# Six first products of batch 1 turned by DMA instead of computed transposed, row loads held by small copies, order refitted

## The chip, the cores and the metric

The kernel runs on one core of one Trainium2 chip. The metric is the device time of one execution in microseconds (us), median of several runs. The core has five engines that run at the same time, each with its own in-order instruction stream: TensorE (PE, matrix products, with its weight loads listed as PEld), VectorE (DVE), ScalarE (ACT), GpSimd (POOL) and SyncE (SP). POOL and SP mainly start DMA transfers here. Engines wait for each other and for transfers through semaphores. An engine that waits keeps everything behind it in its own stream waiting too.

## The reference

Two stages. First a sliding-window attention with sink keys: q, k and v are 4 batches x 8 heads x 768 positions x 64, every query sees the last 128 keys and the first 4 keys.

```python
scores = scale * np.matmul(q, k.transpose(0, 1, 3, 2))
keep = (pos[None, :] < 4) | ((rel >= 0) & (rel < 128))
a = softmax(np.where(keep, scores, -1e9))
x = np.matmul(a, v)            # then heads side by side: x is 3072 x 512
```

Then a dense mixture of four experts, all of them applied to all 3072 tokens:

```python
p = domain_probs / (domain_probs.sum(-1, keepdims=True) + 1e-9)
for e in range(4):
    h = np.maximum(x @ w1[e], 0.0)          # 512 -> 1024
    out += p[:, e:e + 1] * (h @ w2[e])      # 1024 -> 512
```

## The kernel before

**Units.** Everything on PE is in bf16. The tokens of a batch (768) are three pairs of 128-token blocks, so there are 12 pairs (b, g) with b = 0..3 and g = 0..2. One expert on one pair is a unit, written (b, g, e); there are 48. Nearly all units do their matrix products in a seven-product (Strassen-Winograd) form: in place of eight block products there are seven, in the order P1 P5 P6 P2 P7 P3 P4, over sums of blocks of weights and of tokens that DVE, POOL and ACT form beforehand. A unit has two matrix products, the first (x @ w1, with relu) and the second (@ w2).

**The first product, two ways.** Its result H must lie with the hidden index on the partitions, as the second product contracts over it.
- The plain way, `emit_fast` (products at L1208): weights are the stationary operand (128x128), tokens the moving one, so H comes out as it is needed. One of the seven products is 8 matmuls of 128 columns. Gating (relu and the factor p) is done on DVE at L1241, with a row of p copied to all partitions: a "gate tile" that SP loads (`load_gate`, L478) for each such unit.
- The turned way, `emit_turning` (products at L1320): tokens are stationary, weights move, and one product is 2 matmuls of 512 columns. H comes out with tokens on the partitions. There the factor p is one number per partition (`own_gates`, loaded and normalised once by `own_load` and `own_made`), so that gating is either relu and scale on ACT (L1338, L1341) or one step on DVE (L1345). The gated values go into two half buffers, X[0] and X[1], and when the four writes of a unit are done two DMA transposes issued by SP (L1301) turn X[0] and X[1] into H.

**The half buffers of a turned unit.** X[1] serves twice. Its memory first holds the intermediate c5, which is copied out of the accumulator after P5 (ACT, L1373, called "keep" below). DVE adds c5 and the running sum into the accumulator V (L1367, "both"), which frees the accumulator that P7 writes to. DVE then adds P7's result to c5 (L1382). At the end X[1] takes the gated results of P7 and of P4, and only after P4 can X[1] be turned. The next unit that is given this buffer may write its c5 into it only when that transposition has read it.

```python
c5 = X[1].rearrange("p f t n -> p (f t n)").bitcast(FP32).rearrange("p (f n) -> p f n", f=QF)
at["P7"] = at["P3"] = dve(n)                          # "both": P7 may go behind it
return sum(x[0] <= t["pe"] + REST for x in self.resting)   # halves(): which buffers count as free
```

**The planner.** The order of all instructions is written by a planner in the kernel itself, before anything runs: it keeps a clock per engine (`pe`, `act`, `dve`, `pool`, `sp`, `lands`), with fitted costs, and at each step emits what its clocks and due times favour. `later` and `flush` do the same for the steps of DVE and ACT. The real engines then follow the order written, and wait where the plan was too early. A turned unit is opened only when `halves()` finds two buffers whose planned transposition ends no later than `REST` behind PE's planned time. `LANDS` is added to that planned end. The planner gives "keep" no due time after that transposition: the semaphore alone holds it on the chip.

**Who is turned.** `OWN` = 2 says that turned units begin with batch 2; `TURNED_UNITS` = (4, 0) leaves out the first four units of batches 2 and 3: 20 units are turned. Their half buffers are lent from attention tiles that have come to rest (qkn after the last turn of batch 3, then onat and aT) and, after the last plain unit, from the gate tiles (`rest_gates`). Four gate tiles serve the 20 plain units that gate by row.

**Rows of q, k and v.** For each batch six blocks of q and k rows (`load_nat`, L251) and of v rows (`load_v`, L318) are loaded by POOL, 128 KB a transfer. SP then turns q and k by DMA (`turn_nat`, L263) ahead of the scores (L689 onwards). Attention outputs are turned by the same kind of transposition (`turn`, L791). For batches 2 and 3 a GpSimd copy of a freshly turned tile into the two-column tile `held` (L1703), once for each batch, keeps POOL from issuing the first row loads before the last turn of the batch before.

Of the kernel before, what the change touches and what calls it, by code (L numbers as in the profile page):

```python
# [16 lines left out]
def kernel(  # L17
# [12 lines left out]
    nc = tc.nc  # L30
# [23 lines left out]
    GROUPS = [  # L54
        [(0, 0, 2), (1, 1, 1)],
        [(1, 2, 1), (2, 2, 2), (3, 3, 1)],
        [(3, 4, 1), (4, 4, 2), (5, 5, 1)],
    ]

    NGATE = 4  # L60
    TURN_ABOUT = 1
    OWN = 2
    TURNED_UNITS = (4, 0)
    EXPERTS = {(1, 0): (0, 2, 1, 3), (1, 1): (3, 2, 1, 0), (1, 2): (3, 2, 1, 0), (2, 2): (2, 0, 3, 1), (3, 1): (3, 2, 1, 0)}
    FIRST = 1
    START = {0: (1, 0), 1: (0, 2), 2: (0, 0), 3: (1, 0)}
    MIX = 6
    SHARE_OF = (1.01, 0.92, 0.96)
    LEAD = (1.01, 0.99)
    DUE = 1.9  # L70
    LOW_PRODUCT = 2.9
    LOW_SECOND = 2.7
    HIGH_PRODUCT = 1.9
    EARLY = -0.01
    MASK = 5000
    GATE = 800
    GATE0 = 300
    FORM = 6000
    TOKEN = 3000
    MARGIN = 500  # L80
    HOLD = 0
    FULL = 7
    STEP0 = 0.03
    READY = 40
    REST = 3000
    LANDS = 0
    SCALED = 300
    SHARED = 2
    MARGIN1, MARGIN2 = 4000, 14000
    OWNED_READ = 152  # L90
    WIDE = 2
    OPEN = 2.5
    SOON = 34000
    NEARLY = 2
# [5 lines left out]
    ONE = 2  # L100
    HOLDS = 2
    MORE = 2
    BOTH = 1
    PAIR = 0
    OVER = 4
    ALONE = 2.0
    BEHIND = 1500
    CHORES = 3
    BIASED = 1
# [19 lines left out]
    def act(cols, *deps):  # L129
        at = max([t["act"], *deps])  # L130
        t["act"] = at + max(196, 68 + cols / 1.23)
        return at + max(350, 205 + cols / 1.2)

    def dve(cols, *deps, rate=0.96, fixed=157):
        at = max([t["dve"], *deps])
        t["dve"] = at + fixed - 85 + cols / rate
        return at + fixed + 35 + cols / rate

# [60 lines left out]

    landed = {}  # L200
    ROW = {64: 12.8, 128: 22.6, 256: 41.7, 512: 79.8, 1024: 156.2}

    def lands(key, rows, cols, *deps):
        issued = pool(0, *deps, fixed=880)
        at = max(t["sw"], issued + 1500)
        t["sw"] = at + rows * ROW[cols] / 16
        landed[key] = t["sw"] + 900
        moved.append([key, at, t["sw"], ROW[cols]])

# [249 lines left out]

    gate_sb = {}  # L460
    gate_tiles = [consts.tile([P, 2, 2, P], FP32, name=f"gates{i}") for i in range(NGATE // 2)]

# [8 lines left out]
    def load_gate(pair, e):  # L471

        i = len(gate_sb) % NGATE
        x = gate_tiles[i // 2][:, i % 2]
        if FIRST <= len(gate_sb) < NGATE:
            nc.vector.memset(x[0:1, 0, 0:1], 0.0)
            dve(1, fixed=150)
        nc.sync.dma_start(  # L478
            out=x.rearrange("p t n -> p (t n)"), in_=gate_rows[pair, e].rearrange("t n -> (t n)").partition_broadcast(P),
        )  # L480
        gate_sb[pair, e] = x
        sp(takes=300)

# [26 lines left out]
    for tb in (2, 3):  # L510
# [18 lines left out]
    LOW = 32768.0  # L529
    low = [lent[:, 5 * P:8 * P], lent[:, 8 * P:12 * P]]  # L530
    nc.vector.tensor_scalar(
        out=low[0].rearrange("p (n q) -> p n q", n=3)[:, 0::2], in0=two, scalar1=LOW, scalar2=-LOW, op0=ALU.mult, op1=ALU.add,
    )
    nc.vector.tensor_scalar(out=low[0][:, P:2 * P], in0=own, scalar1=-LOW, scalar2=None, op0=ALU.mult)
    nc.vector.memset(low[0][0:NSINK, 0:2 * P], 0.0)
    nc.vector.reduce_sum(
        out=sel2, in_=ident.rearrange("p (n c) -> p n c", c=32)[:, :, 0:2 * NSINK].rearrange("p n (a j) -> p n a j", a=2), axis=AX.X,
    )
    x = low[1].rearrange("p (n c q) -> p n c q", n=2, c=2)
    nc.scalar.activation(out=x[:, :, 0], in_=two, func=AF.Copy, scale=-LOW)  # L540
    nc.scalar.activation(out=x[:, :, 1], in_=two, func=AF.Copy, scale=LOW, bias=-LOW)
    mask0 = consts.tile([P, 3 * P], BF16, name="mask0")
    mask1 = consts.tile([P, 4 * P], BF16, name="mask1")
    made = []

    def make_mask(i):
        def run(engine):
            x = (mask0, mask1)[i]
            if i:
                nc.scalar.activation(out=x, in_=low[i], func=AF.Copy, scale=1 / LOW, bias=1.0)  # L550
                act(4 * P)
            else:
                nc.vector.tensor_scalar(out=x, in0=low[i], scalar1=1 / LOW, scalar2=1.0, op0=ALU.mult, op1=ALU.add)
                dve(3 * P)
            made.append(i)
        later(("dve", "act")[i], (24000.0, 11700.0)[i], 8000, run)
# [132 lines left out]
    def scores(b, hp, g, more=False):  # L689
# [10 lines left out]
        if biased:  # L700
            for ph in range(2):
                nc.tensor.matmul(sps[ph][:, 0:w], lhsT=ident, rhs=low[min(g, 1)], start=True, stop=False, skip_group_check=True)
            pe(2 * w, ready, n=2)
# [18 lines left out]
        if b == 0:  # L722
            part = join(2, masked)
        else:
            def mask_both(at):
                def run(engine):
                    nc.vector.tensor_mul(a, a, m[:, None, :].to_broadcast([P, 2, w]))  # L727
                    masked(dve(2 * w, rate=1.92))
                later("dve", at, MASK, run)
            part = join(2, mask_both)  # L730
        for ph in range(2):
            def run(engine, ph=ph):
# [8 lines left out]
                def mask_one(engine):  # L741
                    nc.vector.tensor_mul(a[:, ph], a[:, ph], m)
                    part(dve(w, rate=1.92))
# [216 lines left out]
    class Mixture:  # L960


        def __init__(self):
# [13 lines left out]
            mine = [u for u in self.order if u[0] >= OWN]  # L977
            self.turning = set(mine[TURNED_UNITS[0]:len(mine) - TURNED_UNITS[1]])
            self.gated = [u for u in self.order if u not in self.turning]
            self.G, self.resting = {}, []  # L980
            self.T, self.T_at, self.fast, self.finished = {}, {}, {}, set()
# [43 lines left out]
        def opened(self, b, g, e):  # L1025
# [11 lines left out]
            def complete(at):  # L1037
                self.H_at[b, g, e] = at
                self.finished.add((b, g, e))
                if (b, g) >= PAIRS[0]:  # L1040
                    self.waiting.append((b, g, e))
                    load_gates()
                    if not TURNED_UNITS[1] and self.gated[-1] == (b, g, e):
                        self.rest_gates()
# [39 lines left out]
        def emit_first(self, what, ready):  # L1084
# [56 lines left out]
            def run(engine):  # L1141
# [5 lines left out]
                part(at)  # L1147
            later("dve", end, GATE0, run)

# [32 lines left out]
        def emit_fast(self, u, m, ready):  # L1182
# [40 lines left out]
            def gated(dst, src, half_, ready, slack, slot=None, then=None):  # L1223
# [16 lines left out]
                def run(engine):  # L1240
# [5 lines left out]
                    if then:  # L1246
                        then(at)
                later("dve", ready, slack, run)

# [35 lines left out]
        def emit_turning(self, u, m, ready):  # L1285
# [47 lines left out]
            def gated(k, s, src, ready, slack, slot=None, then=None):  # L1333
                gate = own_gates[:, 2 * ((b - OWN) * NG + g) + s, e:e + 1]

                def run(engine):
                    if engine == "act":
                        nc.scalar.activation(out=src, in_=src, func=AF.Relu)  # L1338

                        def scaled(engine):  # L1340
                            nc.scalar.mul(X[k][:, :, s], src, gate)  # L1341
                            done(act(n))
                        later("act", act(n), SCALED, scaled)
                        return
                    nc.vector.tensor_scalar(out=X[k][:, :, s], in0=src, scalar1=0.0, scalar2=gate, op0=ALU.max, op1=ALU.mult)  # L1345
                    done(dve(n, fixed=OWNED_READ))

                def done(at):
                    if slot is not None:
                        take(slot, at)  # L1350
# [40 lines left out]
        def chore(self):  # L1391
# [40 lines left out]
            def form(engine):  # L1432
                x = steps.pop(0)
                x[0](*x[1:])
                at = dve(QF * P, self.stored[-1] if (b, g) == PAIRS[0] else 0.0, rate=1.92)
                if steps:
                    go(form, self.until(b, g, e, "P6 P7".split()[len(steps) == 2]))
# [128 lines left out]
        def emit_second(self):  # L1566
# [20 lines left out]
            def run(engine):  # L1587
                if e == 0:
                    nc.vector.tensor_scalar(out=dst, in0=op, scalar1=sc, scalar2=None, op0=ALU.mult)
                else:  # L1590
                    nc.vector.scalar_tensor_tensor(
                        out=dst, in0=op, scalar=sc, in1=dst, op0=ALU.mult, op1=ALU.add,
                    )
                acc_free[bank] = at = dve(Dout, fixed=218)
                if e == E - 1:
                    r = (2 * g + s) * P
                    nc.sync.dma_start(out=out[r:r + P, :], in_=dst)
                    self.stored.append(sp(at))
            later("dve", end, 400, run)
            self.since = 0  # L1600
# [36 lines left out]
    work = [sum(NFB * NDB * G * (1 if (b, g) < START[e] else 7 / 8) + NFB * NDB * G * (1 if (b, g) < PAIRS[0] else 7 / 8) for g in range(NG) for e in range(E)) for b in range(B)]  # L1637
    ahead, upto, loaded, wide, rowed = 0, 0.0, 0, 0, 0
    asked = []
# [22 lines left out]
    while mix.more() or att.more():  # L1662
# [28 lines left out]
        if x and t["pool"] < now + 1500 and free_ring(x):  # L1691
            loads.remove(x)
            x[0](*x[1:])
        if turns and (ahead < 2 or not mix.second) and landed.get(("qk", *turns[0]), 1e12) < now and (turns[0][0] <= ahead or turns[0][0] == ahead + 1 and not att.todo):
# [7 lines left out]
            if 0 < b < B - 1 and x[1] == NQB - 1:  # L1702
                nc.gpsimd.tensor_copy(out=held, in_=qkT[b][:, 1, NHP - 1, S - 2:S])  # L1703
                pool(2, turned_at[x])
                nat_loads(b + 1, range(NQB))
                turns += [(b + 1, tb) for tb in range(NQB)]
        flush(now)
        mix.tokens()
# [3 lines left out]
        if ahead + 1 < B and not att.more() and (ahead == 0 or (ahead + 1, 0) in turned_at) and (ahead == 0 or mix.done >= sum(work[:ahead]) * LEAD[ahead - 1]):  # L1712
            ahead += 1
            if ahead == 1:
                own_load()
            elif ahead == 2:
                own_made()
            att = Attention(ahead)
# [79 lines left out]
```

## Time and profile before

| | |
|---|---|
| time, median of 3 runs | 354.05 us (353.97 to 354.15) |
| span of the profiled execution | 351.9 us |
| time outside the span (354.05 less 351.9) | 2.15 us |
| PE busy | 346.2 us, 98% of the span |
| DVE, ACT, POOL busy | 282.8, 208.3, 71.6 us |
| granted TensorE clock | 1.000 |
| matmuls | 3721 |

The profiled execution has no device time of its own beside its span; the span plus 2.15 us is the median by construction, and sums of durations from the profile are set against that. A line of a group reads: line, engine, operation, output and input tiles, shapes, count, then total busy time in us, mean time of one in ns, idle time ahead of the group with what ended it. A PE line's duration of a matmul includes its passage through the array; matmuls that follow each other overlap, so the cost of one is the distance between starts. A line with "SPq" is the issue of a transfer and not its duration.

### The profile page before, as it was taken

The page shows a single profiled execution, that of the slowest core. Times are in us where ns is not written, and L with a number is a line of the kernel's source. Part 1 is how long each engine was busy: PE and PEld are TensorE (multiplying, and loading weights), DVE is VectorE, ACT ScalarE, POOL GpSimd, SP SyncE. Part 2 cuts the span into 40 slices and gives each one's busy share as a digit, 9 for nine tenths or more (in the row PEclk, how much of TensorE's full clock was granted, in tenths as well). Part 3 has the DMA queues.
Part 4 walks back from the last instruction along what each step waited for, and adds up shares of the span by engine and source line. Part 5 has one row for each costly group of instructions (what it writes and reads, how often), then busy time and mean ns, then how long its engine had stood idle before and what let it go on. Part 6 is the DMA issues. An engine that isn't in the chain of part 4 may idle for free.

```text
span 351.9 us, 9351 instructions
## 1 busy us (share of the span) xinstructions
PE 346.2 (98%) x3721; PEld 266.0 (76%) x3721; DVE 282.8 (80%) x672; ACT 208.3 (59%) x476; POOL 71.6 (20%) x89
## 2 busy tenths in 40 slices
PE   8999999999999999999999999999999999999996
PEld 3685769656789998998999886755856676666685
DVE  5886999878999999799898999578768586675740
ACT  6863624447874443647453539689589767666611
POOL 8946114330546206100152000000000000000000
PEclk9999999999999999999999999999999999999999
DMA  9999999999999999920999602545437733545441
GB/s 178 178 188 195 223 214 181 179 160 174 162 147 165 121 145 122 132 64 9 109 173 159 113 32 62 120 101 120 80 91 174 127 89 93 120 120 115 67 120 61
DMA packets 161032, 45.61 MB, mean 130 GB/s; under 512 B 144740, under 2 KB 156996, under 8 KB 160988
## 3 DMA queue, kind: packets, MB, share of 16 engines
q0 software_dynamic: 79104, 17.31, 56.4%
q1 hardware_dynamic: 80828, 27.18, 40.1%
q8 instruction: 29, 0.48, 0.5%
q10 hardware_dynamic: 1056, 0.52, 0.5%
q14 instruction: 15, 0.12, 0.1%
HBM read 38.39 MB, written 6.34 MB: 127 GB/s over the span
## 4 chain that ended last, share of the span: by engine, by line
PE 75%; DMA 19%; POOL 5%; issue 1%; ACT 0%; POOLq 0%; SPq 0%
PE acc L1493 35%; PE cps L1320 17%; PE cps L1208 15%; DMA w<-in_moe_w_dram 12%; DMA qkn<-in_k_dram 4%; DMA qkT<-qkn 3%; PE sps L708 3%; PE od L774 2%; POOL qkn L251 2%; POOL w L331 1%; POOL vx L318 1%; PE hps L1118 1%; PE od L767 1%; POOL w L341 0%; PE acc L1579 0%
## 5 line engine op out<-in xcount | busy, mean ns | idle before, releaser
L1493 PEld LDWEIGHTS <-H 128*128 128x128 bf16 x708 | 66.5, 98 | 17.9 <-issue 1.1
L1493 PE MATMUL acc<-w,H 128*128 128x256 bf16 x420 | 56.9, 273 | 0.0
L733 ACT ACTIVATE aT<-sps 128x512 bf16<-128x512 f32 (+1 forms) x96 | 47.2, 579 | 16.3 <-PE sps L708 16.2
L1208 PEld LDWEIGHTS <-w 128*128 128x128 bf16 x640 | 39.1, 98 | 1.2 <-issue 0.5
L1493 PEld LDWEIGHTS <-S 128*128 128x128 bf16 x320 | 30.3, 98 | 9.5 <-issue 0.8
L1241 DVE SCALAR_TENSOR_TENSOR H<-cps,gates 128x512 bf16<-128x512 f32 x54 | 36.6, 683 | 0.0
L1338 ACT ACTIVATE cps<-cps 128x512 f32<-128x512 f32 x44 | 25.5, 585 | 17.5 <-PE cps L1320 17.0
L1118 PE MATMUL hps<-xT,w 128*128 128x256 bf16 x256 | 31.9, 273 | 0.1
L819 ACT ACTIVATE onat<-od,R 128x64 bf16<-128x64 f32 x108 | 24.9, 324 | 11.4 <-DVE R L801 11.1
L318 POOL DMA_DIRECT2D vx<-in_v_dram x24 | 21.4, 903 | 43.0 <-PE od L774 31.2
L1208 PEld LDWEIGHTS <-vf 128*128 128x128 bf16 x480 | 29.3, 98 | 1.0 <-issue 0.5
L1579 PE MATMUL acc<-w,H 128*128 128x512 bf16 x128 | 29.9, 379 | 0.0
L1493 PE MATMUL acc<-wf,H 128*128 128x256 bf16 (+1 forms) x216 | 29.6, 272 | 0.0
L1118 PEld LDWEIGHTS <-w 128*128 128x128 bf16 x256 | 24.1, 98 | 4.7 <-issue 0.9
L1341 ACT ACTIVATE rest<-cps,own_gates 128x512 bf16<-128x512 f32 x37 | 25.5, 693 | 0.7
L727 DVE TENSOR_TENSOR aT<-aT,mask 128x1024 bf16<-128x1024 bf16 (+1 forms) x36 | 22.7, 640 | 3.1 <-ACT aT L733 2.8
L251 POOL DMA_DIRECT2D qkn<-in_q_dram x22 | 19.7, 896 | 23.3 <-DMA qkT<-qkn 14.7
L1208 PE MATMUL cps<-T,w 128*128 128x128 bf16 x320 | 24.3, 219 | 0.0
L1208 PE MATMUL cps<-xT,w 128*128 128x128 bf16 x320 | 24.1, 219 | 0.0
L1320 PE MATMUL cps<-w,T 128*128 128x512 bf16 x80 | 23.8, 379 | 0.0
L1320 PE MATMUL cps<-vf,T 128*128 128x512 bf16 x80 | 23.6, 379 | 0.0
L1554 ACT COPY osb<-acc 128x256 f32<-128x256 f32 x32 | 12.1, 382 | 19.3 <-PE acc L1493 19.1
(145 smaller groups left out, 673.5 us busy)
## 6 DMA issues: line engine op xcount, KB each, us to landing
w<-in_moe_w_dram POOLq DMA_DIRECT2D x6, 1024.0 KB, 18.4
out_dram<-osb SPq DMA_DIRECT2D x16, 256.0 KB
vx<-in_v_dram POOLq DMA_DIRECT2D x24, 128.0 KB, 6.5
qkn<-in_q_dram POOLq DMA_DIRECT2D x22, 128.0 KB, 6.7
qkn<-in_k_dram POOLq DMA_DIRECT2D x22, 128.0 KB, 7.4
gates<-gate_rows SPq DMA_DIRECT2D x20, 128.0 KB
w<-in_moe_w_dram POOLq DMA_DIRECT2D x4, 256.0 KB, 6.9
w<-in_moe_w_dram POOLq DMA_DIRECT2D x2, 512.0 KB, 11.5
```

The lines of the kernel that those rows point to most:

```text
L251: nc.gpsimd.dma_start(out=both[:, i], in_=src[b, :, tb * P:(tb + 1) * P, :].rearrange("h p d -> p h d"),)
L318: nc.gpsimd.dma_start(out=vx[tb][:, :, 0:D], in_=v[b, :, tb * P:(tb + 1) * P, :].rearrange("h p d -> p h d"),)
L733: nc.scalar.activation(out=a[:, ph], in_=sps[ph][:, 0:w], func=AF.Exp, scale=scale)
L819: nc.scalar.mul(o[:, qi, hp, ph * D:(ph + 1) * D], od[:, qi, ph, 0:D], R[:, qi, ph])
L1118: nc.tensor.matmul(h[:, i].rearrange("p (q n) -> p q n", q=2), lhsT=w1_sb[e][:, db, fb * P:(fb + 1) * P], rhs=xT[b, g][:, :, db], start=(i ...
L1208: nc.tensor.matmul(y[:, f], lhsT=A[:, d, f * P:(f + 1) * P], rhs=T[:, d], start=(m in ("P1", "P5") and f == 0 and d == 0), stop=(d == 1), ...
L1241: nc.vector.scalar_tensor_tensor(out=dst, in0=src, scalar=0.0, in1=gate, op0=ALU.max, op1=ALU.mult)
L1320: nc.tensor.matmul(y.rearrange("p f n -> p (f n)"), lhsT=T[:, d], rhs=A[:, d], start=(m in ("P1", "P5") and d == 0), stop=(d == 1), skip_g ...
L1338: nc.scalar.activation(out=src, in_=src, func=AF.Relu)
L1341: nc.scalar.mul(X[k][:, :, s], src, gate)
L1493: nc.tensor.matmul(y, lhsT=self.operand(b, g, e, m)[:, f], rhs=forms[e][m][:, f, cs], start=(k == 0 and f == 0 and m in (("P1", "P5", "P2" ...
L1579: nc.tensor.matmul(op, lhsT=H[:, fb // QF, fb % QF, s], rhs=w2_sb[e][:, fb, :], start=(fb == 0), stop=(fb == NFB - 1),)
```

## The change

- `OWN` goes from 2 to 1, and `TURNED_UNITS` becomes a mask over the 36 units of batches 1 to 3. 29 units are turned in place of 20: six of batch 1, namely (1,0,2), (1,0,0), (1,1,1), (1,1,0), (1,2,2), (1,2,3), all of batch 2 but (2,1,2), and all of batch 3. The order of experts within pairs (`EXPERTS`) is new. `own_gates` covers 18 blocks of tokens and not 12, and its normalisation (`own_made`) is planned 26 us behind its load and not at the start of batch 2.
- Half buffers: two tiles `row0` and `row1` of their own (`HALVES` = 2) take the place of two gate tiles (`NGATE` 4 to 2). Until batch 3's q and k are turned, they are the only half buffers. Gate loads fall from 20 to 11.
- `REST` goes from 3000 to 4000 ns and `LANDS` from 0 to -1400 ns.
- `hold()`: before each row load (q with k, and v) of batches 2 and 3, a GpSimd copy of two columns of a tile that a planned DVE step has just written (`marked`) into `held`. These are 24 copies.
- The two masks share one tile and are applied in four groups of 256 columns; the first expert's scaling of the plain second product (L1589, four times) goes from DVE to ACT; the order within the first group of scores is swapped.
- The planner's fitted costs and due times are new, so the order of nearly all work after the first few microseconds is another one.

```diff
-        [(0, 0, 2), (1, 1, 1)],
+        [(1, 1, 1), (0, 0, 2)],
-    NGATE = 4
+    NGATE = 2
-    OWN = 2
-    TURNED_UNITS = (4, 0)
-    EXPERTS = {(1, 0): (0, 2, 1, 3), (1, 1): (3, 2, 1, 0), (1, 2): (3, 2, 1, 0), (2, 2): (2, 0, 3, 1), (3, 1): (3, 2, 1, 0)}
+    OWN = 1
+    TURNED_UNITS = (1, 0, 1, 0, 0, 1, 1, 0, 1, 0, 1, 0, 1, 1, 1, 1, 1, 0, 1, 1, 1, 1, 1, 1, 1, 1, 1, 1, 1, 1, 1, 1, 1, 1, 1, 1)
+    EXPERTS = {(1, 0): (0, 1, 2, 3), (1, 1): (3, 1, 0, 2), (1, 2): (2, 0, 3, 1), (2, 2): (3, 1, 2, 0), (3, 1): (2, 1, 3, 0), (3, 2): (0, 2, 3, 1), (2, 0): (0, 2, 1, 3), (0, 2): (2, 0, 3, 1), (3, 0): (2, 3, 0, 1), (2, 1): (3, 2, 0, 1), (0, 1): (1, 2, 3, 0)}
-    SHARE_OF = (1.01, 0.92, 0.96)
-    LEAD = (1.01, 0.99)
-    DUE = 1.9
+    SHARE_OF = (1.09, 0.99, 1.0)
+    LEAD = (1.025, 0.975)
+    DUE = 1.4
...
-    REST = 3000
-    LANDS = 0
+    REST = 4000
+    LANDS = -1400
...
+    OWNS = 26000
+    HALVES = 2
+    HELD = 2
...
+    def marked(at, x):
+        mark[:] = [at, x]
+
+    def hold():
+        nc.gpsimd.tensor_copy(out=held, in_=mark[1])
+        pool(2, mark[0])
...
-        at = max(t["sw"], issued + 1500)
+        at = max(t["sw"], issued + 800)
...
-            self.turning = set(mine[TURNED_UNITS[0]:len(mine) - TURNED_UNITS[1]])
+            self.turning = {u for u, x in zip(mine, TURNED_UNITS) if x}
             self.gated = [u for u in self.order if u not in self.turning]
-            self.G, self.resting = {}, []
+            self.G = {}
+            self.resting = [(0.0, mo.tile([P, QF, 2, P], BF16, name=f"row{i}", tag=f"row{i}", bufs=1)) for i in range(HALVES)]
...
                 if e == 0:
-                    nc.vector.tensor_scalar(out=dst, in0=op, scalar1=sc, scalar2=None, op0=ALU.mult)
+                    nc.scalar.mul(dst, op, sc)
...
             loads.remove(x)
+            if x[0] is not load_w1 and x[0] is not load_w2 and x[1] >= HELD:
+                hold()
             x[0](*x[1:])
```

## The prediction

> **What bounds the kernel now.** I read the first part of the page, then a table of busy time by stretches, PE's waits, and the timeline of single steps.
>
> ```profile
> span 351.9 us, 9351 instructions
> PE 346.2 (98%) x3721; PEld 266.0 (76%) x3721; DVE 282.8 (80%) x672; ACT 208.3 (59%) x476; POOL 71.6 (20%) x89
> ```
>
> ```profile
> 0.00:27.00 27.00, 24.82 (x261) 16.45 (x262) 20.39 (x78) 18.97 (x40) 20.81 (x30) 1.00 1.63 181
> 95.00:195.00 100.00, 100.00 (x1448) 91.85 (x1443) 93.80 (x225) 53.65 (x153) 29.14 (x35) 1.00 1.26 123
> 195.00:270.00 75.00, 75.00 (x710) 53.14 (x709) 60.57 (x143) 53.91 (x115) 0.00 (x0) 1.00 0.41 94
> 270.00:352.00 82.00, 78.72 (x597) 56.68 (x594) 49.16 (x110) 47.01 (x88) 0.00 (x0) 1.00 0.45 104
> ```
>
> The columns are the stretch and its length, then busy time of PE, PEld, DVE, ACT and POOL, the granted clock, the DMA figure (the summed busy share, larger while rows are loaded) and GB/s. From 27 us to the stores at the end PE has no gap. All waits that PE has:
>
> ```profile
> PE acc L584 <- DVE lent L489: 1.4, 1, 1.4
> PE sinks L669 <- DMA qkT<-qkn: 0.3, 1, 0.3
> PE tx L838 <- DVE onat L804: 0.2, 1, 0.2
> ```
>
> 1.9 us in all. So two things can change the time: less work on PE (a small gain), or a new wait on PE (a loss of its whole length, as nothing else ends PE's stream). The clock is 1.00 throughout and is no part of it.
>
> **The work on PE.** The distances between starts give the price of one product in each form.
>
> ```profile
> 151.33 1.06 PE L1208 MATMUL cps<-T,w 128*128 128x128 bf16 x16
> 152.23 0.60 PE L1493 MATMUL acc<-w,H 128*128 128x256 bf16 x4
> 229.91 0.59 PE L1320 MATMUL cps<-w,T 128*128 128x512 bf16 x2
> 230.34 0.59 PE L1320 MATMUL cps<-vf,xT 128*128 128x512 bf16 x2
> ```
>
> Sixteen matmuls of 128 columns take 152.23 - 151.33 = 0.90 us, 56.1 ns each over the whole trace; two of 512 columns take 0.43 us, 216.7 ns each over the trace. A plain product costs 8 x 56.1 = 449 ns, a turned one 2 x 216.7 = 433 ns. Nine units change form, 63 products: 504 x 56.1 - 126 x 216.7 = 28.27 - 27.30 = 0.97 us less. One more idle product (0.11 us) falls into the wait of 1.4 us at the start. This is the only gain on the path.
>
> At this place a page speaks the other way. The Trainium skill, "TensorE: Matmul & The Clock Gate", section "Back-to-back issue gap", says that in a stream of weight loads and matmuls both set the distance, some 81 ns for 128 columns and 131 ns for 512. By it the change would save 504 x 81 - 126 x 131 = 24.3 us, an estimate from that page; the trace's 56.1 and 216.7 do not agree with it.
>
> **The other engines.** DVE loses 27 gating steps of 0.683 us and nine of c5, 18 additions of 0.69 and 0.68, four scalings of 0.746, and gains ten gatings of 0.748, nine of 0.482, and 18 additions in the turned form: about -13.7 us of 282.8. ACT gains 17 pairs of relu and scale (0.585 + 0.693) and four scalings, less some copies: about +20 us on 208.3. Neither comes near PE's 346, so both are costed at nothing; what hides them is PE's own stream, and the cover goes only where PE waits for one of them in a chain, below. POOL gains 24 copies at 0.21 us (the row of the present copy to held), 5 us on 71.6: nothing, unless a copy waits long. Behind it on POOL stand row loads; for those wait SP's turns of q and k, and for these the scores. In the new order the scores of batch 2 start 16 us later (near 132 us, before 116), and those of batch 3 near 191 us, with the last turn of q and k issued about 184 to 186 us and landed some 6 us later: 0, at most 1.7 us, and then only where the wait C below has not moved PE anyway. SP loses nine gate loads of about 0.3 us and gains 18 transpositions at 1.25 us of issue, 20 us more; SP is idle enough, but it is in order, and that matters in C.
>
> **The reuse of the half buffers.** Here the change adds a wait that PE has to sit out. With two half buffers in batches 1 and 2, the next turned unit puts its c5 ("keep", L1373) where the last one's results are being turned. PE's P7 stands behind "both", "both" behind "keep", "keep" behind the transposition, that behind SP's issue, and that behind the gating of the last unit's P4. The chain from the start of that P4 to the new P7, in rows:
> - P4 to SP's issue. The matmuls 0.60, relu 0.585, scale 0.693: 1.88 us at least. Traced: P4 at 231.64, issue at 233.96, 2.3 us, which is typical.
> - Issue to "keep". Alone:
>
> ```profile
> 333.89 2.58 SPq L1301 DMA_TRANSPOSE H<-rest  x2
> 338.12 0.42 DVE L1434 TENSOR_TENSOR S<-H 128x512 bf16<-128x512 bf16 x1 [2.76 <-DMA H<-rest]
> ```
>
> Two issues in 2.58 us, so the second at 335.2, and DVE, which waited for it, starts at 338.12: 2.9 us. Its last packet is 2.26 us behind the issue, so 0.64 us lie behind that packet. With row loads in flight the last packet comes much later: 3.69, 4.56, 8.20 and 9.04 us behind the issues at 107.15, 105.35, 111.59 and 115.68.
> - "keep" 0.59, "both" 0.69, and the hand-overs, at most 0.28 by the rows below (both ends at 237.26): 1.45 to 1.55 us.
>
> ```profile
> 231.95 1.23 SPq L1301 DMA_TRANSPOSE H<-gates  x1
> 235.33 0.59 ACT L1373 COPY gates<-cps 128x512 f32<-128x512 f32 x1
> 236.57 0.69 DVE L1367 TENSOR_TENSOR cps<-gates,cps 128x512 f32<-128x512 f32 x1
> 237.54 0.59 PE L1320 MATMUL cps<-w,T 128*128 128x512 bf16 x2
> ```
>
> Here "keep" comes 3.38 us after the issue, so it waits for nothing. Together 1.88 + 2.9 + 1.45 = 6.2 us at the very least, 2.3 + 2.9 + 1.45 = 6.65 us as a rule. In the present order the shortest distance on PE from such a P4 (or P3, for the other half) to the P7 is 6.8 us, the next 7.2 and 8.0: no wait, as the trace has none. I laid out the new order of PE's instructions at the traced distances (56.1, 110.3, 216.7 ns). Four distances are now critical; the rest are 7.3 us or more. REST and LANDS together let a unit open 2.4 us earlier against the transposition, which is just the difference.
> - **A**, (1,0,2) to (1,1,1): P4 at 121.8, P7 at 131.0, 9.2 us, but nine loads of rows of batch 2 are issued from 115.6 to 123.6. Ends: alone 6.65, no wait; the slowest row, 2.3 + 9.04 + 0.64 + 1.55 = 13.5, 4.3 us. The mean of the four rows, 6.4, gives 10.8: I take 1.6.
> - **B**, (1,1,0) to (1,2,2): P4 at 150.4, P7 at 155.2, 4.7 us. No rows near. Ends: 6.2, 1.5 us; and with the 3.40 us to the last packet of the transposition issued at 146.45, 2.3 + 3.40 + 0.64 + 1.55 = 7.9, 3.2 us. I take 6.65: 1.9. Behind the waiting "keep" on ACT stands the seed copy of (1,2,0), needed by a P6 at 154.7, so PE may stop there already; it is the same wait.
> - **C**, (1,2,3) to (2,0,0): P4 at 177.4, P7 at 183.0, 5.6 us, and on SP the turn of block (3,3) of q and k stands between the unit's two transpositions. It waits for rows whose loads are held until about 173.0. The trace before has q of that block landing 4.2 us after its issue and k 7.3 us (178.70 to 186.04), so the rows land at 178.3 to 181.4, the second transposition is issued 1.3 us later, 179.6 to 182.7, "keep" starts 2.9 to 6.3 us behind that, and P7 is 1.0 to 7.5 us late. I take 3.0, below the middle, as fewer rows are in flight than around 186 us before.
> - **D**, (2,0,0) to (2,0,2): 184.6 to 190.1, 5.5 us. Ends: 6.2, 0.7 us; and with the 4.56 us of 105.35, 2.3 + 4.56 + 0.64 + 1.55 = 9.05, 3.5 us. The last row load is issued near 179 us and lands some 7 us later, before this issue at about 187: near the low end, 0.9.
>
> The sum: 1.6 + 1.9 + 3.0 + 0.9 = 7.4 us of waits, less 0.97, is +6.4 us. The profiled execution's 351.9 us plus 2.15 outside it is the median of 354.05, so 360.5 us.
>
> **The rivals.**
> - Reuse stays hidden (the other side): the gating of P4 comes through DVE in one step of 0.75 us, or transpositions release the buffer sooner than their consumers show, and all four chains fit. Then only the products count: 354.05 - 0.97 = 353.1. For it: no reuse before has a wait. Against it: B's order has relu and scale on ACT, and 4.7 us is below 6.2. It decides where the whole chain is below 4.7 us. Chance 0.15.
> - Nothing measurable: only one chain bites, for about 1 us, and eats the gain: 354.1 us. It needs A, C and D hidden. Chance 0.06.
> - Rows press harder: transpositions among row loads take what the slowest rows show, A 4.3 and C 7.5 with B 1.9 and D 0.9, 14.6 less 1.0: 367.7. For it: the k rows' 7.3 us and the 8.20 and 9.04; against it: the holds spread the loads. Chance 0.08.
> - Narrow products cost their weight load: a load is 98 ns by the profile's groups, and if that set the distance, 504 x 98 - 27.3 = 22.1 us would go: 332.0. Against it stand the 0.90 us for sixteen. Chance 0.01. (It is the mechanism of the page named above.)
>
> **How the numbers follow.** The forecast has 0.70, and is 360.5. Its own range runs from all four at low ends, 3.2 - 1.0, 356.3, to C at its upper end with the others as taken, 365.0. A difference below 0.2%, 0.7 us, can't be told from none. Faster: 0.15 + 0.01 = 0.16; the same: 0.06; slower: 0.70 + 0.08 = 0.78. The range to hold 8 in 10 goes from 352.9 (with the first rival) to 365.0 and leaves out the last two rivals and a little of the forecast's tail.
>
> **What the profile after would show.** Right: matmuls near 3344, L1208 616 and L1320 406 (by the new line numbers), PE busy lower by waits, rows of PE's waits with P7 or P6 of the turned product behind DVE's "both" or ACT's copies, four of them, around 131, 155, 183 and 190 us, and "keep" idle behind DMA H<-row. Wrong: no such PE waits and PE without gaps in 120 to 195 us; or waits in other places, such as scores behind qkT, which would say that the holds cost more than I gave them; or a distance other than 56 and 217 ns.

## The result: slower by 4.7%

The changed kernel takes 370.6 us (367.93 to 372.7, four runs) against 354.09 us (353.97 to 354.15, four runs) on the same chip: a ratio of 1.0465, interval 1.041 to 1.052. The forecast was slower, 360.5 us with a range up to 365.0. The direction and the places were right, the size was not. The profiled execution has a span of 370.3 us, 18.4 more than before.

The same parts of the page, first part and clock row:

```profile
span 370.3 us, 8708 instructions
PE 351.7 (95%) x3344; PEld 253.4 (68%) x3344; DVE 272.7 (74%) x654; ACT 224.7 (61%) x502; POOL 77.1 (21%) x113
PEclk9999999999999979989998999999999999999999
```

DVE lost 10.1 us and ACT gained 16.4 (forecast -13.7 and +20), and neither is the bound. PE has 377 matmuls fewer and yet 5.5 us more of busy time, and the clock row, which was all nines before, has dips at three places. The waits of PE, in the form "who waits, for whom: us in all, times, longest":

```profile
PE cps L1335 <- DVE cps L1383: 10.1, 3, 4.7
PE cps L1223 <- ACT cps L1269: 2.4, 1, 2.4
PE acc L594 <- DVE lent L501: 1.4, 1, 1.4
PE od L781 <- ACT rest L1356: 0.3, 1, 0.3
PE tx L852 <- DVE onat L818: 0.2, 1, 0.2
```

L1335 is the turned product (L1320 before), L1383 is "both" (L1367), L1269 the seed copy of a plain unit. The first two lines are new; they are the four waits A to D. From the starts of PE's matmuls, less what columns at full clock cost: A 4.57 us (ending at 136.1), B 2.59 (164.4), C 4.90 (199.1), D 1.15 (208.7), 13.2 in all.

The rest lies behind three of the waits, at which the granted clock is halved. The table (stretch, length, busy PE, PEld, DVE, ACT, POOL, granted clock, DMA figure, GB/s) is cut where the clock changes and shows the stretch ahead of each halving too:

```profile
130.25:133.66 3.41, 1.43 (x12) 0.82 (x10) 0.26 (x1) 0.00 (x0) 0.00 (x0) 1.00 1.78 177
133.66:137.08 3.42, 0.99 (x3) 0.41 (x3) 1.74 (x4) 2.04 (x4) 0.00 (x0) 0.50 1.35 186
137.08:140.49 3.41, 3.41 (x18) 1.43 (x16) 1.81 (x6) 2.50 (x6) 0.00 (x0) 0.50 1.03 183
160.97:164.38 3.41, 1.01 (x14) 0.55 (x12) 0.93 (x3) 1.09 (x3) 0.00 (x0) 1.00 0.88 164
164.38:167.79 3.41, 3.38 (x21) 2.26 (x21) 2.57 (x8) 1.74 (x3) 0.00 (x0) 0.50 0.04 14
195.10:198.51 3.41, 0.00 (x0) 0.00 (x0) 0.21 (x1) 0.82 (x2) 0.00 (x0) 1.00 1.40 270
198.51:201.93 3.42, 2.88 (x14) 1.53 (x14) 2.87 (x9) 2.63 (x8) 0.00 (x0) 0.50 0.36 79
```

Once the waits end, at 136.09, 164.41 and 199.05, PE works at half the clock for another 4.4, 3.4 and 2.9 us: pairs of 512-column matmuls start 0.85 us apart and not 0.43. That costs 1.93, 1.62 and 1.39 us, 4.9 in all. The sum: 13.2 of waits, 4.9 of half clock, 0.4 of one more small wait at 285 us, 0.6 more at the start, less 0.84 of matmul time is 18.3 of the 18.4 us.

### The profile page after: what moved, and what is told of

The parts are those of the page before. It is cut to its first block, busy times and chain, and to the rows that moved or that the text cites. A ratio compares the mean times of both kernels' runs of the same rounds, so it can differ in the third digit from the quotient of the medians.

```text
span 370.3 us, 8708 instructions
## 1 busy us (share of the span) xinstructions
PE 351.7 (95%) x3344; PEld 253.4 (68%) x3344; DVE 272.7 (74%) x654; ACT 224.7 (61%) x502; POOL 77.1 (21%) x113
## 4 chain that ended last, share of the span: by engine, by line
PE 82%; DMA 10%; DVE 4%; ACT 1%; issue 1%; SPq 0%; POOL 0%; ACTq 0%; POOLq 0%; DVEq 0%
PE acc L1510 30%; PE cps L1335 21%; PE cps L1223 8%; PE acc L1596 7%; DMA H<-row 7%; PE hps L1133 7%; PE sps L718 3%; PE od L788 2%; PE acc L594 2%; DMA qkn<-in_k_dram 2%; DMA qkT<-qkn 1%; PE od L781 1%; DVE aT L756 1%; PE tr L615 1%; DVE cps L1383 1%
## 5 line engine op out<-in xcount | busy, mean ns | idle before, releaser
L1510 PEld LDWEIGHTS <-H 128*128 128x128 bf16 x708 | 67.2, 98 | 22.9 <-issue 2.5
L1510 PE MATMUL acc<-w,H 128*128 128x256 bf16 x420 | 58.4, 276 | 0.0
L1353 ACT ACTIVATE cps<-cps 128x512 f32<-128x512 f32 x61 | 35.5, 587 | 24.8 <-PE cps L1335 23.5
L1335 PE MATMUL cps<-w,T 128*128 128x512 bf16 x116 | 36.1, 396 | 10.1 <-DVE cps L1383 10.1
L1510 PEld LDWEIGHTS <-S 128*128 128x128 bf16 x320 | 30.6, 98 | 9.9 <-issue 0.9
L1335 PEld LDWEIGHTS <-T 128*128 128x128 bf16 x232 | 21.8, 99 | 20.8 <-issue 10.8
L1335 PE MATMUL cps<-vf,T 128*128 128x512 bf16 x116 | 34.0, 379 | 0.0
L1335 PE MATMUL cps<-w,xT 128*128 128x512 bf16 x116 | 33.8, 379 | 0.0
L1510 PE MATMUL acc<-wf,H 128*128 128x256 bf16 (+1 forms) x208 | 28.7, 271 | 0.0
L1133 PEld LDWEIGHTS <-w 128*128 128x128 bf16 x256 | 24.2, 98 | 4.5 <-issue 0.4
L738 DVE TENSOR_TENSOR aT<-aT,masks 128x1024 bf16<-128x1024 bf16 (+1 forms) x36 | 22.7, 640 | 5.9 <-ACT aT L746 5.8
L1376 ACT COPY cps<-cps 128x512 f32<-128x512 f32 x29 | 17.1, 589 | 15.7 <-PE cps L1335 12.0
L1383 DVE TENSOR_TENSOR cps<-row,cps 128x512 f32<-128x512 f32 x14 | 9.7, 695 | 22.1 <-ACT row L1389 15.0
L1335 PEld LDWEIGHTS <-xT 128*128 128x128 bf16 x174 | 16.9, 100 | 11.5 <-issue 1.7
L1223 PEld LDWEIGHTS <-w 128*128 128x128 bf16 x352 | 22.1, 98 | 3.3 <-issue 0.7
L1356 ACT ACTIVATE row<-cps,own_gates 128x512 bf16<-128x512 f32 x32 | 22.4, 699 | 0.6
```

Of the source, the lines that this page charges most:

```text
L738: nc.vector.tensor_mul(x, x, m[:, None, :].to_broadcast([P, 2 if g == 0 else 4, w if g == 0 else 2 * P]))
L1133: nc.tensor.matmul(h[:, i].rearrange("p (q n) -> p q n", q=2), lhsT=w1_sb[e][:, db, fb * P:(fb + 1) * P], rhs=xT[b, g][:, :, db], start=(i ...
L1223: nc.tensor.matmul(y[:, f], lhsT=A[:, d, f * P:(f + 1) * P], rhs=T[:, d], start=(m in ("P1", "P5") and f == 0 and d == 0), stop=(d == 1), ...
L1335: nc.tensor.matmul(y.rearrange("p f n -> p (f n)"), lhsT=T[:, d], rhs=A[:, d], start=(m in ("P1", "P5") and d == 0), stop=(d == 1), skip_g ...
L1510: nc.tensor.matmul(y, lhsT=self.operand(b, g, e, m)[:, f], rhs=forms[e][m][:, f, cs], start=(k == 0 and f == 0 and m in (("P1", "P5", "P2" ...
```

## Experiments

Times are set against the kernel before, timed on the same chip as the run (353.67 to 353.79 us). Chain terms are read from the timelines.

### Which buffer c5 takes

```diff
-                self.G[b, g, e] = [self.half(), self.half()]
+                self.G[b, g, e] = [self.half(), self.half()][::-1]
```

> The changed kernel with the two half buffers of a unit handed out the other way round, so that c5 goes into the buffer whose transposition was issued first. The order of PE's, ACT's and DVE's instructions stays. Theory (PE waits for the reuse of half buffers): all four waits of 4.6, 2.6, 4.9 and 1.2 us shrink; the second and the fourth lie on bare transpositions issued about 1.5 us apart, so they lose about 1.5 us each (to about 1.0 and 0); the third loses most, as the turn of q and k no longer stands ahead of the transposition that counts (to about 1 to 2); the first loses 1.6 to 3. Waits 4 to 7 us in all, time 360 to 364 us. Rival (the waits come from somewhere else, such as rows that land late or the holds): the waits stay above 11 us and the time above 368.

Measured: 359.02 us, ratio 1.0170 (1.0141 to 1.0199), 11.6 us less than the changed kernel by one reversed list. PE's waits:

```profile
PE cps L1335 <- ACT onat L833: 1.4, 1, 1.4
PE sps L718 <- ACT row L1356: 1.2, 1, 1.2
PE cps L1335 <- DVE cps L1383: 0.8, 2, 0.6
PE cps L1223 <- ACT cps L1269: 0.5, 1, 0.5
```

In its trace the waits sum to 4.7 us and the clock is 1.000. B and D are down to 0.6 and 0.4, C to 0.8, A to 0.2; the time is a little below the expected 360 to 364. What is left of A has moved. The other half of the unit now holds the late buffer, and ACT's gating into it waits for that transposition, with PE's scores behind ACT:

```profile
133.21 0.69 ACT L1356 ACTIVATE row<-cps,own_gates 128x512 bf16<-128x512 f32 x1 [2.02 <-DMA H<-row]
133.95 0.32 PE L718 MATMUL sps<-qkT 64*128 64x128 bf16 x3 [1.19 <-ACT row L1356]
```

The 1.4 us at L1335 come the same way, behind a gating that idles 1.42 us for DMA H<-row at 188.43. So the reuse of half buffers is the cause of the waits. Had the scores or PE waited for the rows to land, or for the holds, the four waits would have stayed, since neither is touched here.

### The rows of q, k and v

```diff
+            hs = slice(0, 1 if b >= 2 else H)
+            if b >= 2 and i == 0:
+                nc.gpsimd.memset(both[:, :, 1:], 0.0)
+                hold()
             nc.gpsimd.dma_start(
-                out=both[:, i], in_=src[b, :, tb * P:(tb + 1) * P, :].rearrange("h p d -> p h d"),
+                out=both[:, i, hs], in_=src[b, hs, tb * P:(tb + 1) * P, :].rearrange("h p d -> p h d"),
             )
...
-            nc.gpsimd.dma_start(
-                out=vx[tb][:, :, 0:D],
+            if b < 2:
+                nc.gpsimd.dma_start(
+                    out=vx[tb][:, :, 0:D],
...
```

> The changed kernel with the row traffic of batches 2 and 3 all but taken away: one head of eight of q and k is loaded, the rest of the tile is filled with zeros by GpSimd ahead of the hold, and v is not loaded again; the output is therefore not the reference's. All orders stay. Theory (reuse, lengthened by row loads at the first and the third place): the first wait of 4.6 us goes to 0, the third from 4.9 to about 1, the second and fourth stay near 2.6 and 1.1; time 358 to 362 us. Rival (a transposition takes about 10 us there without the rows, or SP's order makes it): the first and third stay above 3.5 us each, time above 367.

Measured: 360.46 us, ratio 1.0188 (1.0167 to 1.021). A is gone. B is 2.40, C 2.42, D 2.04 (expected 2.6, 1 and 1.1; why D is longer than in the changed kernel is not shown). PE's waits (the lines are five further down in this kernel; L1388 is "both", L1274 the seed copy):

```profile
PE cps L1340 <- DVE cps L1388: 4.1, 2, 2.3
PE cps L1228 <- ACT cps L1274: 2.2, 1, 2.2
```

By this run all of A's 4.6 us and half of C's 4.9 are the rows' work. What is left is the chain without them. Here the second of two transpositions is read 3.3 to 3.6 us behind its issue (at B, C and D 3.6, 3.6 and 3.3), and not 2.9; and at C it is still issued behind the turn of q and k.

In the changed kernel itself, place A looks like this:

```profile
122.33 5.84 SPq L1316 DMA_TRANSPOSE H<-row  x2
122.63 0.90 POOL L263 DMA_DIRECT2D qkn<-in_k_dram  x1
123.62 0.90 POOL L263 DMA_DIRECT2D qkn<-in_q_dram  x1
124.49 0.90 POOL L263 DMA_DIRECT2D qkn<-in_k_dram  x1
134.72 0.58 ACT L1389 COPY row<-cps 128x512 f32<-128x512 f32 x1 [6.85 <-DMA H<-row]
135.34 0.69 DVE L1383 TENSOR_TENSOR cps<-row,cps 128x512 f32<-128x512 f32 x1 [4.83 <-ACT row L1389]
```

The second issue of the pair begins at 123.95 and lasts 4.22 us by itself; "keep" starts at 134.72, 10.8 us later. The loads that were in flight with it suffer as well: the three issued from 122.63 on land 9.6, 12.1 and 13.4 us behind their issue, against a median of 7.3 to 7.7 on the page.

### Both causes away

The last two edits together.

> Both causes taken from the changed kernel at once: half buffers the other way round, and the row traffic of batches 2 and 3 all but taken away (one head of eight of q and k, zeros from GpSimd in the rest, v not loaded again; the output is therefore not the reference's). Theory (reuse, lengthened by the rows, and nothing else): waits of at most 0.8 us at each of the four places, 2 us in all, full clock; time 352.8 to 355.5, the kernel before within 0.5%. Rival (something else in the new order costs time too, such as scores behind ACT): more than 2.5 us of waits at other lines, time 356 to 359.

Measured: 354.52 us, ratio 1.0027 (1.0015 to 1.0039), waits of 1.0 us, clock 1.000, span 352.8. The 16 us are gone but for 0.9. PE's waits, all of them:

```profile
PE acc L599 <- DVE lent L506: 1.4, 1, 1.4
PE cps L1340 <- DVE cps L1388: 0.6, 2, 0.4
PE tx L857 <- DVE onat L823: 0.2, 1, 0.2
```

The first and the third stand in the kernel before as well. So whatever else the new order costs is small: the 0.9 us and the 0.8 us that PE has less to do make 1.7 us, and 1.0 of it are the waits. As the rows are needed, this is no kernel to use; it says that even with both causes away the change is no faster than the kernel before.

### The holds

```diff
     def hold():
-        nc.gpsimd.tensor_copy(out=held, in_=mark[1])
         pool(2, mark[0])
```

> The changed kernel without the 24 copies that hold the row loads; the planner still counts them, so that all other orders stay. Theory (reuse): four waits at the same places; the second and fourth, which have no rows beside them, stay near 2.6 and 1.1 us, and the first and third move with where the rows then lie, by up to 4 us either way; time 364 to 374 us. Rival (the holds make the waits): the waits fall below 4 us in all and the time to 354 to 360.

Measured: 372.65 us, ratio 1.0525 (1.0506 to 1.0544). The four waits stay, 4.29, 2.43, 4.70 and 0.66 us, and two of 0.9 us come in at 115 and 152 us. The second transposition at A is issued at 124.50 and read at 135.31, 10.8 us again. The holds neither make the waits nor cure them. With them or without them the row loads of place A are issued up to 124 us, beside the transpositions.

### SP's order at the third place

```diff
                         def turn(at):
+                            turned_units.add((b, g, e, k))
...
-        if turns and (ahead < 2 or not mix.second) and landed.get(("qk", *turns[0]), 1e12) < now and (turns[0][0] <= ahead or turns[0][0] == ahead + 1 and not att.todo):
+        if turns and (turns[0] != (3, 3) or (1, 2, 3, 1) in turned_units) and (ahead < 2 or not mix.second) and landed.get(("qk", *turns[0]), 1e12) < now and (turns[0][0] <= ahead or turns[0][0] == ahead + 1 and not att.todo):
```

> The changed kernel with one step of SP moved: the turn of block (3,3) of q and k is issued behind the second transposition of unit (1,2,3) and not between its two; the order of the other engines changes only for a few steps behind that place. Theory (SP's in-order queue is part of the third wait): the transposition that counts is issued about 1.5 to 2 us earlier, the third wait falls from 4.9 to about 3, the others stay at 4.6, 2.6 and about 1; time 366 to 370 us. Rival (the rows in flight alone make the third wait, and SP's place does not matter): it stays above 4.5 us.

Measured: 368.52 us, ratio 1.0390 (1.034 to 1.0441); the third wait is 4.31 us, the first 3.83, the second 2.30, the fourth not seen. Neither theory's number for the third wait came out. The transposition that counts is issued at 191.11 and read at 198.05, 6.9 us later; in the changed kernel the issue was at 192.23 and the reading at 197.69, 5.5 us later. Two row loads are issued at 191.07 and 191.93 here, and at 189.58 and 190.45 in the changed kernel, so they now fall together with this transposition. That they took back most of what SP gave fits these times and is not shown apart. Between these two traces SP's place is worth 0.6 us with rows in flight; how much without them was not tried.

### Later opening

```diff
-    REST = 4000
-    LANDS = -1400
+    REST = 0
+    LANDS = 3000
```

> The changed kernel with REST 0 and LANDS 3000: the planner opens a turned unit only when its buffers' transpositions have landed with 3 us to spare. The turned units, the holds and the work on PE stay, only the order moves; the distances from a unit's P4 (or P3) to the P7 that needs its buffer become 11.9, 10.4, 14.3 and 9.1 us in place of 9.2, 4.7, 5.6 and 5.5. Theory (reuse): the second, third and fourth wait vanish, of the first 0 to 2.6 us are left; time 353 to 357 us. Rival (the turned units of batch 1, the holds or SP's longer queue cost the time in themselves): waits of 5 us or more stay, time above 360.

Measured: 372.07 us, ratio 1.0542 (1.0498 to 1.0587), no better than the changed kernel and 15 us beyond what I expected. The three waits on L1383 are gone, as the theory says. Others stand in their place:

```profile
PE od L788 <- DVE aT L738: 3.8, 5, 1.8
PE acc L1510 <- DMA H<-row: 3.3, 1, 3.3
```

Values now wait for exp and mask (L788 behind L738), and products of the second stage come up before H is turned (L1510 behind the transposition itself). A likely reason for the first is that a unit which may not open leaves PE fewer products to put between attention steps; no run shows it apart. The waits of this plan are in other places; it did not get rid of them.

The same with the buffers handed out the other way round, first with LANDS 0 alone:

```diff
-    LANDS = -1400
+    LANDS = 0
...
-                self.G[b, g, e] = [self.half(), self.half()]
+                self.G[b, g, e] = [self.half(), self.half()][::-1]
```

> The changed kernel with the half buffers handed out the other way round and LANDS 0 in place of -1400: the planner opens turned units 1.4 us later against the transposition, and the four distances become 10.4, 7.4, 9.7 and more than 10.5 us (they were 10.6, 6.5, 6.9 and 6.7 with the swap alone, 9.2, 4.7, 5.6 and 5.5 in the changed kernel). Theory (reuse alone): waits of at most 2.5 us, at the first place, none behind it; time 353.3 to 356.5. Rival (a plan that opens turned units later has fewer products to put between attention steps, and PE waits for exp and masks instead): waits of scores and values of 3 us and more, time 357 to 368.

Measured: 362.1 us, ratio 1.0230 (1.0200 to 1.0261); and with REST 3000 too:

```diff
-    REST = 4000
+    REST = 3000
```

> The same with REST 3000 too (both constants as in the kernel before): distances 10.4, 8.7, 9.6 and 7.7 us. Theory (reuse alone): time 353.3 to 356.5, at or below the run with LANDS 0 alone. Rival (fewer products between attention steps): longer than that run, 358 to 370, with PE's waits at scores and values.

Measured: 364.94 us, ratio 1.0316 (1.0293 to 1.0338). Both are above the swap alone. The theory of reuse alone misses both; the rival has the order of the times, but not the line. In the first of the two PE's largest new waits are

```profile
PE cps L1335 <- DVE cps L1383: 3.2, 1, 3.2
PE acc L1510 <- DMA H<-row: 2.3, 1, 2.3
```

and not scores and values. "Keep" no longer waits there (188.23, no idle time). What waits is DVE's sums for the second stage, and with them "both", which stands behind them on DVE:

```profile
183.91 2.61 SPq L1316 DMA_TRANSPOSE H<-row  x1
190.54 0.42 DVE L1450 TENSOR_TENSOR S<-H 128x512 bf16<-128x512 bf16 x1 [4.90 <-DMA H<-row]
192.81 0.69 DVE L1383 TENSOR_TENSOR cps<-row,cps 128x512 f32<-128x512 f32 x1
193.55 1.01 PE L1335 MATMUL cps<-w,T 128*128 128x512 bf16 x2 [3.23 <-DVE cps L1383]
```

It is the same late transposition, issued among row loads at 183.91 and read at 190.54, seen by another reader.

### Waits put into the kernel before

Is the half clock a matter of the wait, or of what runs beside it at those places? In the kernel before, in batch 3, where no rows are loaded:

```diff
+    STALLS = {(3, 0, 0): 14, (3, 0, 2): 8, (3, 1, 3): 20, (3, 1, 1): 11, (3, 2, 0): 24, (3, 2, 2): 17}
...
                     u["both"](act(n))
+                    if (b, g, e) in STALLS:
+                        nc.gpsimd.tensor_copy(out=held, in_=c5[:, 0, 0:2])
+                        for _ in range(STALLS[b, g, e]):
+                            nc.gpsimd.tensor_copy(out=held, in_=held)
+                        x = self.T[b, g]["P7"][:, 0, 0:2]
+                        nc.gpsimd.tensor_copy(out=x, in_=x)
```

> The kernel before with six waits put into PE's stream in batch 3, where nothing else holds PE: behind the c5 copy of six turned units GpSimd makes a chain of 14, 8, 20, 11, 24 and 17 small copies (two columns each) and then rewrites two columns of that unit's P7 operand with themselves, so that P7 waits for the chain. Results do not change. By 0.2 to 0.25 us for one copy the six waits are about 2.4, 1.0, 4, 1.7, 5 and 3 us, near 265, 277, 291, 304, 318 and 333 us. Theory (a long gap on PE also halves the granted clock for some us behind it): the waits of 3 us and more are each followed by matmuls at double distance (433 ns for 512 columns) for 2 to 4.5 us, 1 to 2 us lost beside the wait; those below 2.4 us are not; the time is the sum of the waits plus 4 to 6 us. Rival (the slow matmuls behind the waits of the changed kernel come from the DMA traffic around 136, 165 and 199 us, or from what runs beside): no slow matmuls here, the time is before plus the waits alone.

Measured: 379.05 us, ratio 1.0708 (1.0693 to 1.0724), 25.3 us more than before. The waits are 2.8, 2.1, 4.1, 1.9, 5.0 and 3.4 us, 19.4 in all. Stretches at the third wait (294.0 to 298.0) and at the sixth (346.8 to 350.2):

```profile
293.71:297.12 3.41, 0.39 (x4) 0.10 (x2) 0.00 (x0) 1.27 (x2) 2.60 (x14) 1.00 0.24 82
297.12:300.53 3.41, 2.52 (x8) 1.19 (x9) 1.36 (x3) 0.00 (x0) 0.67 (x4) 0.50 0.00 0
300.53:303.94 3.41, 3.41 (x13) 1.81 (x12) 1.57 (x4) 1.54 (x3) 0.00 (x0) 0.50 0.26 88
344.90:348.31 3.41, 2.07 (x16) 1.23 (x13) 1.76 (x5) 1.83 (x3) 2.12 (x11) 1.00 0.68 154
348.31:351.73 3.42, 1.52 (x10) 0.99 (x11) 0.78 (x2) 0.38 (x2) 1.42 (x9) 1.00 0.00 0
```

Behind the waits of 4.1 and 5.0 us PE works at half clock for 5.9 us each, behind the others not at all. So a wait is enough; no row loads are needed. The 25.3 us less 19.4 are 5.9 us, about 3 for each half-clock stretch, as half of 5.9. I had expected one behind the wait of 3.4 us too, and it did not come, while B's wait of 2.6 us in the changed kernel was followed by one.

The traces show why: what counts is where a wait falls. In each of the eleven traces of this case the clock changes only at times that lie whole multiples of 3.41 us apart, a grid that lies elsewhere in each run (133.66, 140.49, 164.38, 167.79, 198.51 and 201.93 in the changed kernel; 297.12, 303.94, 331.25 and 338.07 here). Once the clock is full, every stretch of that grid in which PE is busy for 1.43 us or less is followed by half clock, and none with 1.46 us or more is. Full clock comes back behind a stretch with 2.63 us or more, and not behind one with 2.55 or less. The wait of 3.4 us is cut in two by the grid, which leaves 2.07 and 1.52 us of work on either side; B's 2.6 us lie in one stretch, with 1.01 us of work. By these figures a single wait in an otherwise busy stream halves the clock never below about 1.9 us and always above about 4 us, and between them its place on the grid decides (an estimate from 3.41, 1.43 and 1.46).

## Why the prediction was right and wrong

**Right: what bounds, what is gained, where it is lost.** PE's matmul time fell by 0.84 us at the same prices (0.97 forecast, less the idle product). The 24 us estimated from the Trainium skill, "TensorE: Matmul & The Clock Gate", section "Back-to-back issue gap", are not borne out. The four waits stand where they were put, A, B, C and D, in that chain (PE behind "both", "both" behind "keep", "keep" behind the transposition), with B seen first at the P6 behind the seed copy, as said. (For D the profile names PE as the last to release "keep", but "keep" starts 3.3 us behind the issue at 204.03, just as in the run with few rows.) The other costs at nothing held, though the terms listed for DVE add up to about -15.7 and not -13.7 if a step of c5 costs 0.683 like the other gating steps.

**Wrong: the size.** In the prediction's own terms:
- A was taken as 1.6 us from "the mean of the four rows, 6.4" with 0.64 behind the last packet, so 7.0 us from issue to "keep". It was 10.8, above even the upper end of 9.7, and the wait 4.57. The step that failed is the mean over the four rows: 115.68 (9.04 us), right behind a burst of loads, was the row that A is nearest to. A's last packet came 8.9 us behind the issue, and "keep" 1.9 us behind that packet and not 0.64. The kernel before already shows what such a burst does: its row loads issued at 113.57, 114.44 and 115.30 landed 10.8, 13.3 and 16.3 us behind their issue.
- B was 2.59 for 1.9. "Alone 2.9 us" was one pair at 335 us; here it was 3.8, inside the bounds given.
- C was 4.90 for 3.0. "Below the middle, as fewer rows are in flight" does not hold: 5.5 us from an issue at 192.23, above the middle of the 2.9 to 6.3 given. The run with few rows puts half of it on the rows, the other half on the chain without them.
- D was 1.15 for 0.9.
- Together 13.2 for 7.4 us. This is 5.8 of the 11.6 us that separate 360.5 from the 372.07 of the profiled execution.
- The other large part had no term at all: 4.9 us at half clock behind A, B and C. The prediction said "the clock is 1.00 throughout and is no part of it", and read from a kernel without waits what holds only without waits. The Trainium skill, "TensorE: Matmul & The Clock Gate", section "What's actually happening", has it: a hardware monitor halves PE's clock after an idle window of some 3.4 us, and the window runs freely. The traces agree on the length, 3.41 us, and on the free run. They add that the window need not be idle throughout: PE was busy for 1.43 us of the one ahead of A's halving and for 1.01 us of the one ahead of B's.

**The rivals.** "Reuse stays hidden" and "nothing measurable" are out. "Rows press harder" (A 4.3, C 7.5, in all 367.7) was the nearest: right for A, too much for C, and its time came near only as the clock made up the difference. The range ended at 365.0 because it let just one of the unknown lengths go to its end (all four upper ends together are 18.5 us) and had no clock in it.

**Open.** Runs of the changed kernel differ by 4.8 us (367.93 to 372.7) where those before differ by 0.2. Their mean clocks go from 0.994 to 0.980, the fastest run having the highest. This fits dips that come or stay away from one run to the next, as a grid that lies elsewhere in each run would make them, but only one execution was traced. Whether another plan with two half buffers could gain anything is not shown.

## What to carry over

When PE is never idle, a change that narrows the time between a buffer's release and its next use is better priced by the slowest transfer that the profile shows at such a place than by the mean, since PE takes the whole of it: at A the slowest row gave 4.3 us and the mean 1.6, and 4.57 were measured (at C the slowest, 7.5 for 4.90, was too much). Add the clock: in the changed kernel and in the one with added waits each halving cost 1.4 to 3 us more behind its wait. A wait of 2.3 us (the second in the run with SP's order moved) brought one, and an added one of 3.4 us did not. And before moving the plan, look at which of two buffers goes to the earlier reader: reversing that list was worth 11.6 us here, while opening later brought waits at other readers.

## What I had not expected of the hardware

- A DMA transposition of one half buffer, read 2.9 us behind its issue at 335 us, was read only 10.8 us behind it among row loads, and the issue alone took 4.22 us in place of 1.23. The row loads beside it landed after up to 13.4 us.
- PE's granted clock changes only on a grid of 3.41 us that lies elsewhere in each run. One stretch of it with 1.43 us of work or less halves the clock for the next 3.41 or 6.83 us, in which PE, busy again, worked at half speed for 2.9 us (C) to 5.9 us (the added waits).
